# A new prologue order with token tiles normalised on GpSimd, and a new tile table

## The chip, the core and the metric

The kernel runs on one core of one Trainium2 chip. The core has a matrix engine (TensorE, PE in the profile; PEld is its weight load), VectorE (DVE), ScalarE (ACT), GpSimd (POOL) and SyncE (SP), which here only starts transfers. SBUF is the working memory, PSUM the memory of eight banks into which PE writes. The metric is the device time of one execution in microseconds (us). Three runs of the kernel before took 742.13, 742.68 and 742.68.

## The reference

One layer normalisation feeds two branches that are added to the input: attention with 32 query heads and a single key and value head (16 wide), and a dense layer with gelu.

```python
def _A_ref(x, wq, wk, wv, wo):                      # x is 1 x 2048 x 512
    H = 32; Dh = D // H                             # 16
    q = (x @ wq).reshape(B, S, H, Dh).transpose(0, 2, 1, 3)
    k = x @ wk
    v = x @ wv
    scores = jnp.einsum("bhqd,bkd->bhqk", q, k) * (Dh ** -0.5)
    p = _softmax(scores, axis=-1)
    o = jnp.einsum("bhqk,bkd->bhqd", p, v)
    return o.transpose(0, 2, 1, 3).reshape(B, S, H * Dh) @ wo

def _B_ref(x, w1, b1, w2, b2):                      # 512 -> 1792 -> 512
    h = _gelu(jnp.einsum("bsd,df->bsf", x, w1) + b1)
    return jnp.einsum("bsf,fd->bsd", h, w2) + b2

xn = _layernorm(x, axis=-1)
return x + _A_ref(xn, A_wq, A_wk, A_wv, A_wo) + _B_ref(xn, B_w1, B_b1, B_w2, B_b2)
```

The tensors are bfloat16. The output has to match within the usual error of bfloat16, which leaves room for an approximate exponential.

## The kernel before

*How it is planned.* The Python text first writes down every instruction with the engine, the buffers it reads and writes, an expected duration (`occ`), an expected latency until others see its result (`lat`) and, for some, a due time (`due`). Then `Prog.schedule` plays the five engines through in Python: each engine takes, among the instructions whose inputs are there, the one with the smallest due time (`min(cand, key=self.due)`), or, without one, with the smallest ready time plus `allow`. The order that comes out, and the waits between engines that it needs, are written into the program; on the chip every engine works through its own list in that order. So an edit of a due time or of an expected duration changes the order of instructions and nothing else. DMAs have a stream of their own and keep the due times written at their place.

*Main part.* Scores are made in 2048 tiles of 128 keys by 512 queries (4 query blocks x 8 head groups x 16 key tiles x 4 heads). Three tiles make a unit (683 units), one PSUM bank each; two halves of six banks are used in turn. `scores` (L984) is PE's product of KT and QT. A unit's tiles are then exponentiated either by ACT (`exp`, L1007, all its tiles of the unit in one instruction of 512 columns a tile) or, one tile in 3.6, by DVE with an approximation: `p1` (L1038) turns scores into int16 in `Dt`, and `close_batch` makes three more shifted copies of a batch of up to six tiles. Two of the three additions are DVE instructions over the whole batch (L1085), the third is one instruction a tile (L1081) that the planner puts on GpSimd or DVE. PE multiplies a tile of ACT with V once and a tile of DVE five times, with five scaled copies of V (L1051). `DTAB` has a letter for each unit that says which of its tiles go to DVE; the letters o, t, A, B and X also close the batch. `HP` and `YP` are the units at which the dense layer's two products are placed between the scores, as side work of PE (L681) whose results DVE takes out of PSUM.

*Prologue.* Before the first scores everything below has to be there; token tiles are 128 rows of x, sixteen of them, loaded in eight transfers.

1. Statistics of a token tile: on DVE, `bn_stats` and `bn_aggr` (L770, L784), or on ACT in two passes with accumulators (L767, L777). `LN_B` groups the tiles and says who does it ('d' or 'a').
2. For each group ACT computes the reciprocal deviation as exp(-0.5 ln(var)): L789, L791. Where ACT will normalise a tile, GpSimd makes the negated mean and its product first (`nm`, `nmr`, L773, L788, L793).
3. The normalised tile in `xn` (a part of `ub`, eight slots): `XN_ENG` has one letter a tile, ACT (L803) or DVE (L806, L809).
4. PE transposes a tile in four pieces (L821) into a PSUM bank; pairs of tiles (`TR_B`) are copied to `xnT` by ACT (L826) or DVE (L828) in one instruction of 128x1024.
5. PE projects keys (`K_B`, copied to KT by ACT, L840), and keys and values a token tile at a time (`v_tiles`). ACT squares the keys (L851, L855) and DVE reduces them (L852); the maximum over all keys (L908, L909, L911) goes through PE to `ibi` (L913), a bound that the scores of every row need.
6. The first query group: PE, then a copy (L865) and a square (L866) on DVE; with `ibi` DVE finishes QT (L872). The first `scores` wait for that.
7. DVE copies V out of PSUM (L919, L921) and GpSimd writes its five scaled copies (L925). GpSimd also writes all constants, zeroes QT (L719) and V1 (L733), and copies the first weights (L721, L886).

Due times of the prologue are given before as landing time of the tile (`LAND`) plus a constant for the kind of instruction (`DU`).

Of the kernel before, what the change touches and what calls it, by code (L numbers as in the profile page):

```python
# [64 lines left out]
DTAB = "oto00t0t..2otttt.0o.022t2tt22o.t0t.o.t0.o.2o200.t2.oo2t.o2o20.ooo0.0.2o2ot.00o2t0.00.20200t.2.oo.t202t0o22.22t.2tt.0.2o2o2.0o00.00oot.t2ooot0.00o.2oot.2oo002o.2tt.02ot.2t20..2t2t22t22xxXB2tt0.otot02to.0o02o0.0.o002tt202.2ttt..o0o20t22t0.0020o2t0202.20o0.o.tt.t.202o.t0o00o2o..o2tt22t22.2t.000o.20t..022tt2..0t.0t00t2t0.02o22.t02tt22.2o0.0o..to.22Bo..2to.0to0to.0oot020t0o2o22..tot00o.o0002o0t..02ot00o22..tt2020o202.oo0o.0202..oo20o0to.2to0.000t.2.o22to00o00.o2.t00o22.20.2tt..02o0022ot..202o.0o02t0ooo.220tot22ABXXB.ttt2o000o22..o0t22o.t0t2o2.o2o0ot02..2t0t222o2o.ot0.t0t2.0.t2o2o0o20o.202t0t2.0..2tt2o.2.to0.B0o0oo.0020t2t20t.t02o.2o0t0t..020o2o22ttt.t22t..ot2.t22t.222to.0oo.2.t.."  # L65
# [14 lines left out]
HP = ((53.36313,15,65.7807,136.33728,36.21312,67.40194,19.02609,18.84758,51,110.61621,34.41429,141,69.06988,99.66158),(149.70144,81.67117,82.37987,103.81985,165,0,0,0,0,0,0,0,0,0),(275.55645,309,280.33349,316.4732,250.53442,309,294.19346,284.369,335.7432,441.67367,320.02286,269.73972,453.75804,500.42149),(465.20765,488,484.21727,494.32464,439.21827,0,0,0,0,0,0,0,0,0))  # L80
YP = ((190.97923,183,219.34307,231),(345.97678,369.69708,381,411.01734),(538.21525,518.41703,557.35214,582.08895),(589.35156,621,652.22097,657))
# [9 lines left out]
Q_DUE = 16.0  # L91
# [4 lines left out]
XN_ENG = "adddddadddddaadd"  # L96
LN_B = (((0,), 'd'), ((1,), 'a'), ((2, 3, 4), 'd'), ((5,), 'a'), ((6, 7), 'd'), ((8, 9, 11), 'd'), ((13,), 'a'), ((14, 15), 'd'), ((10,), 'd'), ((12,), 'd'))
TR_B = (((0, 2), 2, 'a'), ((2, 4), 0, 'a'), ((4, 6), 1, 'd'), ((6, 8), 0, 'a'), ((8, 10), 0, 'd'), ((10, 12), 2, 'a'), ((12, 14), 1, 'a'), ((14, 16), 0, 'd'))
K_B = (((0, 2), 4), ((2, 6), 4), ((6, 10), 4), ((10, 12), 4), ((12, 16), 4))
V_B = ((0, 4), (4, 8), (8, 14), (14, 16))  # L100
NVA = 14
KV_ORD = (1, 2, 3, 4, 0)
# [444 lines left out]
def bass_parallel_sum__grouped_kv_mqa__dense_activation_gelu__prompt_kernel(  # L547
# [33 lines left out]
    with ExitStack() as es:  # L581
# [248 lines left out]
        def tr(a, b):  # L830
            return [("xnT", ti) for ti in range(a, b)]
# [618 lines left out]
```

## Time and profile before

| | |
|---|---|
| Runs | 742.13, 742.68, 742.68 us, median 742.68 |
| Profiled execution | 742.0 us, of which the span from first to last instruction is 740.3 us |
| First exponential of ACT starts | 24.09 us after the span's start |
| Granted TensorE clock | 1.000 |
| Instructions | 22182 |

The profile is one execution, recorded by the hardware. A row of a group reads: line of the kernel, engine, operation, tile written <- tiles read, shapes, count, then busy time, mean nanoseconds of one, and idle time of the engine before it with what ended it. A row of the order of time reads: start, duration, engine, line, operation, names, shapes, count. A row of a stretch gives its bounds and length, then busy time and count of instructions for PE, PEld, DVE, ACT and POOL, the granted clock, the share of the DMA engines and GB/s. The chain of waits follows the last instruction back to whatever released it, step by step, so a step's length there is the time until the next one could start, not the length of its record.

### The profile page before, as it was taken

To read this page: it belongs to the slowest core of one execution; us is meant where nothing else is said; L and a number is where in the kernel's file an instruction comes from. 1 tells how busy PE (TensorE), PEld (TensorE's weight loads), DVE (VectorE), ACT (ScalarE), POOL (GpSimd) and SP (SyncE) were. 2 spreads that over 40 slices of the span, in tenths; PEclk is the share of its full clock that TensorE was granted. 3 is DMA by queue.
4 is the path that set the end of the run, shared out by engine and by line. 5 is a ranking of instruction groups with operands and counts; after the bars stand their busy time and mean duration, and the time that the engine had idled before them with its cause. 6 is when DMAs were issued, how large, how long until landed. Compare 5 with 4: busy or idle time off the path is not lost.

```text
span 740.3 us, 22182 instructions
## 1 busy us (share of the span) xinstructions
PE 724.7 (98%) x9145; PEld 228.2 (31%) x9145; DVE 726.8 (98%) x1411; ACT 728.0 (98%) x759; POOL 393.7 (53%) x547
## 2 busy tenths in 40 slices
PE   7999999999999999999999999999999999999998
PEld 4323233222343223322232332232233222233222
DVE  8899999999999999999999999999999999999996
ACT  8999999999999999999999999999999999999997
POOL 5545565555415564555655546556643566644542
PEclk9999999999999999999999999999999999999999
DMA  9200100100020020101101010100100101101110
GB/s 312 67 15 16 33 8 17 25 10 20 10 48 15 5 54 17 26 23 30 25 13 35 25 39 18 24 23 9 26 17 20 30 23 38 31 24 25 27 25 27
DMA packets 36252, 23.57 MB, mean 32 GB/s; under 512 B 17768, under 2 KB 32568, under 8 KB 36152
## 3 DMA queue, kind: packets, MB, share of 16 engines
q1 hardware_dynamic: 35096, 22.12, 11.7%
q8 instruction: 73, 1.20, 0.7%
q14 instruction: 27, 0.22, 0.1%
q10 hardware_dynamic: 1056, 0.03, 0.1%
HBM read 13.28 MB, written 2.35 MB: 21 GB/s over the span
## 4 chain that ended last, share of the span: by engine, by line
ACT 63%; PE 32%; DVE 4%; DMA 0%; issue 0%; SPq 0%
ACT E L1007 62%; PE pAll L1051 15%; PE pAll L984 9%; PE pAll L681 7%; DVE stats L770 1%; DVE Dt L1038 1%; DVE Dt L1085 1%; DMA x_sb<-in_A_x_dram 0%; PE pAll L675 0%; DVE Dt L1081 0%; DVE ub L806 0%; ACT xnT L826 0%; ACT ub L803 0%; DVE Of L1132 0%; PE pAll L1411 0%
## 5 line engine op out<-in xcount | busy, mean ns | idle before, releaser
L1007 ACT ACTIVATE E<-pAll 128x1024 bf16<-128x1024 f32 (+1 forms) x678 | 675.2, 1191 | 2.3 <-PE pAll L984 2.2
L1081 POOL TENSOR_SCALAR Dt<-Dt 128x512 int16<-128x512 int16 x463 | 354.1, 765 | 311.2 <-DVE Dt L1085 137.3
L1051 PE MATMUL pAll<-Dt,V 128*32 128x512 bf16 x2850 | 422.4, 383 | 1.1 <-DVE Of L1132 1.1
L1038 DVE TENSOR_SCALAR Dt<-pAll 128x512 int16<-128x512 f32 (+1 forms) x555 | 377.3, 696 | 1.9 <-PE pAll L984 1.1
L1085 DVE TENSOR_SCALAR Dt<-Dt 128x1024 int16<-128x1024 int16 (+7 forms) x542 | 294.4, 571 | 0.1
L1051 PE MATMUL pAll<-E,V 128*32 128x512 bf16 x1478 | 276.0, 385 | 0.8 <-DVE Of L1132 0.8
L984 PE MATMUL pAll<-QT,KT 32*128 32x512 bf16 x2048 | 267.2, 384 | 4.4 <-ACT E L1007 2.8
L984 PEld LDWEIGHTS pAll<-QT,KT 32*128 32x128 bf16 x2048 | 66.5, 90 | 275.0 <-ACT E L1007 261.4
L1051 PEld LDWEIGHTS pAll<-Dt,V 128*32 128x32 bf16 x2850 | 112.4, 95 | 117.0 <-issue 70.9
L681 PE MATMUL pAll<-xnT,w_sb 128*32 128x512 bf16 x896 | 118.9, 382 | 0.0
L1051 PEld LDWEIGHTS pAll<-E,V 128*32 128x32 bf16 x1478 | 65.1, 94 | 51.3 <-issue 37.4
L681 PE MATMUL pAll<-w_sb,ub 128*32 128x512 bf16 x448 | 70.3, 382 | 0.0
L681 PE MATMUL pAll<-w_sb,x_sb 128*32 128x512 bf16 x448 | 68.4, 382 | 0.0
L681 PEld LDWEIGHTS pAll<-xnT,w_sb 128*32 128x32 bf16 x896 | 33.6, 95 | 21.1 <-issue 9.7
L681 PE MATMUL pAll<-wop,oTp 128*32 128x512 bf16 x192 | 31.4, 384 | 0.0
L1081 DVE TENSOR_SCALAR Dt<-Dt 128x512 int16<-128x512 int16 x107 | 27.5, 284 | 0.0
L1160 POOL TENSOR_TENSOR oTp<-OfP,rbP 128x256 bf16<-128x256 f32 x24 | 18.7, 790 | 7.5 <-DVE Dt L1085 3.9
L1215 DVE TENSOR_SCALAR ub<-pAll,b1T 128x512 bf16<-128x512 f32 x28 | 20.8, 742 | 0.2
L681 PE MATMUL pAll<-xnT,wq_sb 128*32 128x512 bf16 x256 | 20.0, 383 | 0.3 <-DVE ub L1215 0.3
L681 PEld LDWEIGHTS pAll<-w_sb,x_sb 128*32 128x32 bf16 x448 | 18.2, 95 | 4.8 <-issue 2.7
L681 PEld LDWEIGHTS pAll<-w_sb,ub 128*32 128x32 bf16 x448 | 18.5, 95 | 3.8 <-issue 2.0
L1132 DVE COPY Of<-pAll 128x512 f32<-128x512 f32 x24 | 16.3, 681 | 0.0
(122 smaller groups left out, 255.9 us busy)
## 6 DMA issues: line engine op xcount, KB each, us to landing
w_sb<-in_B_w_dram SPq DMA_DIRECT2D x2, 1792.0 KB, 13.2
OfP<-Of SPq DMA_DIRECT2D x96, 32.0 KB, 2.0
rbP<-rden_rows SPq DMA_DIRECT2D x96, 32.0 KB, 1.8
x_sb<-in_A_x_dram SPq DMA_DIRECT2D x8, 256.0 KB, 4.3
x_sb<-in_A_x_dram SPq DMA_DIRECT2D x16, 128.0 KB, 2.3
QT<-qp SPq DMA_DIRECT2D x124, 16.0 KB, 1.8
out_dram<-x_sb SPq DMA_DIRECT2D x15, 128.0 KB, 2.0
OfP<-Of SPq DMA_DIRECT2D x56, 16.0 KB, 1.8
```

Of the source, the lines that this page charges most:

```text
L681: add("pe", lambda e, c=c, j=j: e.matmul(o[c, :], l[:, c], rh, start=start, stop=stop, tile_position=(0, 32 * j)), r, [(k, j) for k in w] ...
L770: dve(lambda e, ti=ti, c=c: e.bn_stats(stats[:, c, :], x_sb[:, ti, :]), r=[("x", ti)], w=[("st", ti)], n=511, due=land(ti) + DU["sd"])
L984: ins = e.matmul(o, l, rh, start=True, stop=True, tile_position=(q0, 0))
L1007: o = act(lambda e: e.activation(E[:, s0:s0 + na, :], bank(b0, na).rearrange("p (a n) -> p a n", a=na), ACT.Exp, scale=LN2 / 128.0), w=[B( ...
L1038: op = dve(lambda e: e.tensor_scalar(Dt[:, s:s + n, :], bank(bk, n).rearrange("p (a n) -> p a n", a=n), float(127 * 128) + SPL_D, SPL_MIN, ...
L1051: add("pe", lambda e, a, b: e.matmul(pO[32 * j:32 * j + 32, :], V1[:, v, kt, :], rhs, start=a, stop=b, tile_position=(0, 32 * j)), r=r + [ ...
L1081: add("pool", lambda e, d=d, k=k: e.tensor_scalar(d, d, 1.0, float(k), ALU.mult, ALU.add), [], [(("D", base[o > 0] + q), o)], occ=PL_OCC, ...
L1085: dve(lambda e, d=view(o, nb), q=view(i, nb), k=k: e.tensor_scalar(d, q, float(k), None, ALU.add), r=keys(i), w=keys(o), n=nb * n * TBW, m ...
L1132: dve(lambda e: e.tensor_copy(Of[:, i, :], pO), w=["O", ("Of", i)], allow=0.0)
L1160: "pool", lambda e, c=c: e.tensor_tensor(oTp[0:n, sl, c], OfP[0:n, s, c], rbP[0:n, s, c], ALU.mult),
L1215: dve(lambda e: e.tensor_scalar(ubs[tb % 2][:, ft, :], pM, b1T[:, ft:ft + 1], None, ALU.add), r=["b1T"], w=M4 + [ukey(tb, ft)], n=TBW + 57 ...
```

## The change

All in one edit:

- `XN_ENG` gets a third letter, p, for GpSimd: eleven tiles are normalised there, two on ACT (4 before), three on DVE (12 before).
- `LN_B`: thirteen groups instead of ten; two tiles instead of three have their statistics on ACT.
- `TR_B`: the copies to `xnT` are on ACT for two pairs, on DVE for four; the last two pairs are split ('s'), half of the columns by each of them from two banks. Keys of `xnT` in the planner become halves, so that PE can start a projection on the first half.
- `K_B` groups the keys by 4, 2, 2, 4, 4 tiles (before 2, 4, 4, 2, 4). `NVA` is 10 instead of 14: the squared keys are reduced in two pieces by DVE.
- The first QT copy goes to ACT (`Q_ENG`), the zeroing of QT is split between DVE and GpSimd (`Q0_SPLIT`), one of the five scaled V copies goes to DVE (`KV_DVE`).
- Every instruction ahead of the first scores gets a due time of its own (`PRO_DUE`, 308 numbers, set by the new `rank`); `DU` and the due times written at the instructions are gone. Expected durations and latencies of the prologue are changed.
- `DTAB`, `HP` and `YP` are replaced by other tables.

In the old table 570 tiles go to DVE, in 271 batches (99 of one tile, 92 of two, 47 of three, 23 of four, 6 of five, 4 of six); in the new one 571, in 250 batches (83, 79, 47, 26, 5, 10). Both leave ACT 678 instructions. 418 of the 683 letters differ.

```diff
-DTAB = "oto00t0t..2otttt.0o.022t2tt22o.t0t.o.t0.o.2o200.t2.oo2t.o2o20.ooo0.0.2o2ot
...
+DTAB = "2to00o2.o0.t0222t.o.0to200t.22.0o020.o0.t.2t000o2.t.2t000t.o002.o020.202.o
...
-XN_ENG = "adddddadddddaadd"
-LN_B = (((0,), 'd'), ((1,), 'a'), ((2, 3, 4), 'd'), ((5,), 'a'), ((6, 7), 'd'), ((8, 9, 11), 'd'), ((13,), 'a'), ((14, 15), 'd'), ((10,), 'd'), ((12,), 'd'))
-TR_B = (((0, 2), 2, 'a'), ((2, 4), 0, 'a'), ((4, 6), 1, 'd'), ((6, 8), 0, 'a'), ((8, 10), 0, 'd'), ((10, 12), 2, 'a'), ((12, 14), 1, 'a'), ((14, 16), 0, 'd'))
-K_B = (((0, 2), 4), ((2, 6), 4), ((6, 10), 4), ((10, 12), 4), ((12, 16), 4))
-NVA = 14
-KV_ORD = (1, 2, 3, 4, 0)
-KV_DVE = ()
+XN_ENG = "papppdpppppdapdp"
+LN_B = (((0,), "d"), ((1,), "a"), ((2, 3), "d"), ((4,), "a"), ((5,), "d"), ((6,), "d"), ((7, 12), "d"), ((8,), "d"), ((9,), "d"), ((11,), "d"), ((13,), "d"), ((10, 14), "d"), ((15,), "d"))
+TR_B = (((0, 2), 1, "d"), ((2, 4), 0, "a"), ((4, 6), 2, "d"), ((6, 8), 1, "a"), ((8, 10), 1, "d"), ((10, 12), 2, "d"), ((12, 14), 0, "s"), ((14, 16), 0, "s"))
+K_B = (((0, 4), 4), ((4, 6), 4), ((6, 8), 4), ((8, 12), 4), ((12, 16), 4))
+NVA = 10
+KV_ORD = (4, 1, 0, 3, 2)
+KV_DVE = (2,)
+XP_OCC = 0.75
+PRO_DUE = (10.3,11.34,29.84,9.77,-0.16,19.38,19.64,19.9,13.73,13.99,14.25,11.64
...
+Q_ENG = "ad"
+Q0_SPLIT = 4
...
+    def rank(self):
+        s0 = next(o.idx for o in self.ops if o.kind == "S")
+        due = iter(PRO_DUE)
+        for op in self.ops[:s0]:
+            op.due = (op.due or 0.0) if op.stream != op.eng else next(due)
+
     def schedule(self):
         ops = self.ops
+        self.rank()
...
+        for g0, g1, f, kw in ((0, Q0_SPLIT, dve, dict(n=Q0_SPLIT * TBW // 2)), (Q0_SPLIT, NGR, setup, dict(occ=0.24 * (NGR - Q0_SPLIT)))):
+            if g0 < g1:
+                f(lambda e, g0=g0, g1=g1: e.memset(QT[:, g0:g1, :].rearrange("p g n -> p (g n)").bitcast(f32), 0.0),
...
+                f = lambda e: e.tensor_scalar(xn[:, ti % 8, :], x_sb[:, ti, :], mean, rs, o, ALU.mult)
+                rw = dict(r=[("x", ti), ("rstd", b), key], w=[("u", 0, ti % 8)])
+                if XN_ENG[ti] == "p":
+                    setup(f, occ=XP_OCC, **rw)
+                else:
+                    dve(f, n=245, **rw)
...
+            parts = ((0, 2, bk, "a"), (2, 4, (bk + 1) % 3, "d")) if eng == "s" else ((0, DT, bk, eng),)
+            for d0, d1, bk, eng in parts:
+                m = (d1 - d0) * n
+                pT = bank(bk)[:, 0:m * 64].bitcast(bf)
...
+            if Q_ENG[0] == "a":
+                act(lambda e: e.activation(QT[:, 0, :], bank(bk), ACT.Copy), w=[B(bk)] + q_rows(0))
```

More of the change, by code (lines that the diff above doesn't have):

```diff
@@ L659, in B @@
             return ("bank", b)
-        dlat = [0.16, 0.23]
+        dlat = [0.135, 0.2]
         def dve(fn, r=(), w=(), n=TBW, mode=1, allow=1.0, **kw):
@@ L907, in bass_parallel_sum__grouped_kv_mqa__dense_activation_gelu__prompt_kernel @@
                 q_first(7)
-        dve(lambda e: e.tensor_reduce(kmx[:], kmax[:], AX.X, ALU.max), r=[("kmax", 0), ("kmax", NVA)], w=["kmx"], n=40, due=0.0)
+        dve(lambda e: e.tensor_reduce(kmx[:], kmax[:], AX.X, ALU.max), r=[("kmax", ti) for ti in range(NT)], w=["kmx"], n=40, due=0.0)
         add("pe", lambda e: e.transpose(bank(3)[0:1, 0:P], kmx[:], ident_f[:]), r=["kmx", "ident_f"], w=[B(3)], occ=0.12, lat=0.22,
```

146 lines of the change are left out of this document (70 added, 76 removed).

## The prediction

> **What bounds the kernel now.** I read the totals first, then the stretches of time, then the chain of waits through the start, then single engines by shape.
>
> ```profile
> PE 724.7 (98%) x9145; PEld 228.2 (31%) x9145; DVE 726.8 (98%) x1411; ACT 728.0 (98%) x759; POOL 393.7 (53%) x547
> ...
> 24.00:733.00 709.00, 703.01 (x8909) 215.49 (x8910) 706.04 (x1349) 706.29 (x703) 381.25 (x499) 1.00 0.10 23
> ```
>
> Three engines are busy 98% each; the second row (PE, PEld, DVE, ACT, POOL in that order) says that from 24 to 733 us VectorE (DVE) and ScalarE (ACT) leave under 3 us open. Busy time alone does not name the bound, since records of neighbours overlap. The order of time of DVE shows by how much:
>
> ```profile
> 399.49 0.68 DVE L1038 TENSOR_SCALAR Dt<-pAll 128x512 int16<-128x512 f32 x1
> 400.09 0.28 DVE L1085 TENSOR_SCALAR Dt<-Dt 128x512 int16<-128x512 int16 x1
> 400.29 0.68 DVE L1038 TENSOR_SCALAR Dt<-pAll 128x512 int16<-128x512 f32 x1
> 400.89 0.41 DVE L1085 TENSOR_SCALAR Dt<-Dt 128x1024 int16<-128x1024 int16 x1
> 401.22 0.68 DVE L1038 TENSOR_SCALAR Dt<-pAll 128x512 int16<-128x512 f32 x1
> ```
>
> A 0.68 record is followed after 0.60, a 0.28 after 0.20, a 0.41 after 0.33: a step is the record less 0.08, and the next instruction starts at that moment each time. So DVE is truly full in the main part, and what is taken from its work there comes off the time. ACT has a little hidden air: one exponential of 128x1024 costs it 0.87 when fed, as PE's releases show (an ACT of one unit frees the next group of scores at 726.83 and again at 727.70), against a mean of 675.2/678 = 0.996 per instruction.
>
> ```profile
> L1007 ACT ACTIVATE E<-pAll 128x1024 bf16<-128x1024 f32 (+1 forms) x678 | 675.2, 1191 | 2.3 <-PE pAll L984 2.2
> ...
> 726.83 0.10 PEld L984 LDWEIGHTS pAll<-QT,KT 32*128 32x128 bf16 x3 [0.42 <-ACT E L1007]
> ...
> 727.70 0.10 PEld L984 LDWEIGHTS pAll<-QT,KT 32*128 32x128 bf16 x3 [0.42 <-ACT E L1007]
> ```
>
> Ahead of it lies a prologue in which no attention tile can start: all sixteen token tiles must be normalised, transposed and projected, since the row bound is a maximum over all keys. By stretches and by the chain:
>
> ```profile
> 0.00:5.00 5.00, 3.26 (x16) 2.26 (x16) 1.47 (x5) 2.19 (x4) 4.31 (x19) 1.00 0.64 161
> 5.00:10.00 5.00, 2.93 (x22) 2.01 (x21) 5.00 (x15) 4.72 (x15) 4.25 (x20) 1.00 1.10 348
> 10.00:15.00 5.00, 3.91 (x63) 2.82 (x61) 5.00 (x15) 5.00 (x14) 1.30 (x7) 1.00 1.03 398
> 15.00:20.00 5.00, 4.30 (x59) 2.62 (x55) 4.51 (x13) 4.85 (x14) 0.52 (x2) 1.00 1.10 352
> ...
> 7.56 0.08 DVE mv L784
> 7.64 0.58 DVE stats L770
> ...
> 8.68 0.95 DVE ub L806 x3
> ...
> 16.19 0.29 ACT lnv L789
> ...
> 17.19 0.09 ACT rstd L791
> 17.29 0.70 ACT ub L803
> 17.99 1.82 ACT xnT L826 x2
> ...
> 22.79 0.81 DVE QT L872
> ...
> 24.09 0.70 DVE Dt L1038
> ```
>
> From 5 to 20 us DVE and ACT are full and GpSimd (POOL) is nearly empty after 10. The chain runs along DVE (statistics 0.58 + 0.08 a tile, a normalised tile 0.95/3 = 0.317), at the end over ACT, and the first exponential and the first L1038 start together at 24.09. Whatever pulls that moment forward moves everything behind it.
>
> **The change part by part.** *Prologue, DVE.* Nine of its twelve normalised tiles go to GpSimd (letters d: 12, then 3): 9 x 0.317 = -2.85. The copy of the first QT goes to ACT:
>
> ```profile
> 16.69 0.69 DVE L865 CAST QT<-pAll 128x512 bf16<-128x512 f32 x1
> ...
> 17.29 0.68 DVE L828 COPY xnT<-pAll 128x1024 bf16<-128x1024 bf16 x1
> ```
>
> so -0.60 (16.69 to 17.29). Added: one tile of statistics moves from ACT to DVE, +0.66; the copies of xnT out of PSUM on DVE go from three whole ones to four and two halves, a whole one 0.68 less the 0.08, so +0.60, a half about 0.34 (an estimate: half of it and a fixed part), so +0.68; a second small reduce of kmax, about +0.15 (an estimate: the shortest DVE records beside it are 0.17). Sum -3.45 + 2.09 = -1.36, call it -1.4. The zeroing of half of QT (128x1024) comes to DVE too; a 128x256 memset took 0.27 there, so about 1.1, and it lies in the 2.4 us in which DVE waits for the first tokens. If that cover were gone, it would cost its 1.1.
>
> ```profile
> 1.20 0.27 DVE L718 MEMSET oTp<- 128x256 uint32 x1
> ...
> 3.87 0.69 DVE L770 BATCH_NORM_STATS2 stats<-x_sb 128x6 f32<-128x512 bf16 x1 [2.40 <-DMA x_sb<-in_A_x_dram]
> ```
>
> *Prologue, ACT.*
>
> ```profile
> L777 ACT ACTIVATE oTp<-x_sb,nm 128x512 bf16<-128x512 bf16 x3 | 2.1, 710 | 0.0
> ...
> 21.45 0.17 DVE L908 TENSOR_REDUCE kmx<-kmax 128x1 f32<-128x16 f32 x1
> ```
>
> Two normalised tiles fewer (-2 x 0.70), one tile of statistics fewer (two passes like L777, -1.4), copies out of PSUM from five whole ones (1.82/2 = 0.91 each) to two and two halves (near -1.8), against three more pairs of logarithm and exponential (thirteen groups for ten, 0.29 + 0.09 each, +1.1) and the QT copy (+0.6): about -2.9. ACT falls by more than DVE, so DVE sets the prologue and I count its -1.4. The bounds: 0 if the new order leaves as much new idle as work goes; -2.2 if DVE runs gapless from the second pair of tokens (statistics of before began at 4.95): it then has 13 statistics (8.6), 3 tiles (0.95) and copies (3.1) left, the last copy ends near 17.6, and an estimated 1.6 us of projection, square and reduce bring the key maximum (L908) to 19.2, where it started at 21.45.
>
> *Prologue, GpSimd.* No row has this operation (pointer scalars, bf16 to another tile). The nearest is the same instruction on 512 two-byte elements; farther ones are 256 f32 elements in short rows (L925, 0.93 apart) and a pointer scalar on 128 elements (L932).
>
> ```profile
> L1081 POOL TENSOR_SCALAR Dt<-Dt 128x512 int16<-128x512 int16 x463 | 354.1, 765 | 311.2 <-DVE Dt L1085 137.3 <-PE pAll L1051 59.0 <-DVE Dt L1038 49.4
> ...
> 21.81 4.65 POOL L925 TENSOR_SCALAR V<-oTp 128x256 bf16<-128x256 f32 x5 [5.31 <-DVE oTp L919]
> ...
> 5.14 0.20 ACT L791 ACTIVATE rstd<-lnv 128x1 f32<-128x1 f32 x1
> ...
> L932 POOL TENSOR_SCALAR sel8R<-sel,R x1: 887/887/887, 26.4 to 26.4; 128x128 bf16<-128x128 bf16 x1
> ...
> L1081 POOL TENSOR_SCALAR Dt<-Dt x463: 619/621/1797, 28.0 to 729.1; 128x512 int16<-128x512 int16 x155
> ```
>
> Bounds: 0.62 (median, alone) and 2.95 (if 0.2 of the 0.887 is fixed, 0.69 for 128 elements, times four, plus 0.2). I take the mean 0.77, since width, element size and two arithmetic steps agree with it. Eleven tiles are 8.5; the small steps between them and the two weight copies are about 1.8 (an estimate, nine records of 0.2); the set-up work that GpSimd did by 10 us was 8.56, less 0.9 for the half QT, of which 4.5 fit ahead of the first reciprocal deviation (L791, 5.14 + 0.20), so 3.2 are left over. From 5.3 this ends at 5.3 + 8.5 + 1.8 + 3.2 = 18.8 at worst, and near 15.6 if the left-over set-up stands behind. The transposes of the last tiles are queued behind it on PE. The last normalised tiles of before ended at 18.95, so GpSimd hides, with little to spare. No DMA is added and none moved.
>
> *End of the prologue.* One of five scaled copies of V goes from GpSimd (0.93 apart) to DVE and may stand between the small steps there, beside GpSimd's other copies: 0 to 0.9, taken +0.3. The dues, the latencies of the planner and the moved memset of epsc change no instruction; they cost nothing but order, which the bounds above hold.
>
> *Main part.* The tile letters give 571 instead of 570 tiles to DVE; the count of ACT's exponentials stays 678 and one tile less is worth at most 0.4 there. A batch of tiles on DVE ends with two additions (L1085); the letters make 250 batches of 271, so 42 instructions fewer.
>
> ```profile
> L1085 DVE TENSOR_SCALAR Dt<-Dt 128x1024 int16<-128x1024 int16 (+7 forms) x542 | 294.4, 571 | 0.1
> ...
> L1085 DVE TENSOR_SCALAR Dt<-Dt 128x2048 int16<-128x2048 int16 x115 | 78.2, 683 | 0.0
> L1085 DVE TENSOR_SCALAR Dt<-Dt 128x1024 int16<-128x1024 int16 x191 | 77.6, 418 | 0.1
> ...
> L1081 DVE TENSOR_SCALAR Dt<-Dt 128x512 int16<-128x512 int16 x107 | 27.5, 284 | 0.0
> ```
>
> (542 = 2 x 271 bears the count out.) From 1024 to 2048 elements a record grows by 0.265, so 0.153 is fixed, 0.073 of it after the overlap: 42 x 0.073 = -3.1. The added tile costs 0.60 (L1038) and 3 x 0.133 (its share of the additions) = +1.0. DVE's balance is -2.1, and DVE is the full engine. What the table does besides is not in the rows: the third kind of addition, L1081, ran 463 times on GpSimd and 107 times on DVE at 0.20 a step, split by the planner; 20 more or fewer on DVE are +-4. Larger batches also hold DVE longer at a time (a 3072 step instead of a 1024 one) while a score bank waits to be emptied. I take -1.8, a little less than the balance, with -6 and +3 as bounds. The new places of the projection groups (HP, YP) move work of PE and DVE within the same count: inside those bounds.
>
> *Sum.* -1.4 + 0.3 - 1.8 = -2.9. The profiled execution took 742.0 (span 740.3, 1.7 around it): 739.1. The median of the runs, 742.68, lies 0.7 above the profiled one: **739.8**.
>
> **A rule to weigh.** L1081 on GpSimd takes 0.62 alone, yet up to 1.80, and the long ones stand beside DVE's L1085:
>
> ```profile
> 439.72 1.26 POOL L1081 TENSOR_SCALAR Dt<-Dt 128x512 int16<-128x512 int16 x1 [0.18 <-DVE Dt L1038]
> ...
> 439.56 0.95 DVE L1085 TENSOR_SCALAR Dt<-Dt 128x3072 int16<-128x3072 int16 x1
> ```
>
> The statistics, copies out of PSUM and casts showed no such thing, but GpSimd was at work beside only a part of them. The Trainium skill ("SBUF — State Buffer", "Who interferes with whom") says that GpSimd and a VectorE instruction which uses both SBUF ports, or has two SBUF inputs, shut each other out for a whole instruction. By that rule DVE's three own normalised tiles, the square of QT and the small copies of V would stand behind GpSimd's tiles. The trace agrees for L1081 and cannot show it for the new pairing. The first rival prices it from rows.
>
> **The rivals.** *GpSimd's tiles hold up DVE in the prologue (11%).* The instructions in question are about seven (three tiles, one square, three copies into V1). Each can wait up to the 0.62 of a GpSimd tile, half of it on average: 7 x 0.31 = 2.2 in place of the 0.3: -1.4 + 2.2 - 1.8 = -1.0, so 741.7. For: the pair above. Against: statistics are most of DVE's work there, and nothing in their thirteen records varied.
>
> *The prologue comes, the table gives nothing (17%).* DVE's saving goes into waits on late scores. For: DVE and ACT waited only 3 us in 709, so nearly any other order has more to lose than to win. Against: fewer instructions on the full engine. -1.4 + 0.3 = -1.1: 741.6. If besides 23 additions of L1081 come to DVE (8%), +4.6 - 2.1 more: +1.4, 744.1.
>
> *GpSimd is too slow for eleven tiles (slower, 8%).* Place: its queue, from the first deviation at 5.3 to the last tile; everything behind it, transposes, projections, key maximum, waits. Price: with c us a tile it ends at 5.3 + 1.8 + 11c when the set-up stands behind. It decides against the change from 18.95 + 1.8 on (the old end and the main part's saving), c = 1.24. At c = 1.5 it ends at 23.6, 4.65 later than before: +4.65 - 1.8 = +2.85, 745.5. For: L932, whose rate gives 2.95, and L925, 0.93 for half the elements. Against: 463 records of the same width at 0.62 to 0.77; L932 also ran beside two L1085.
>
> *More than the sum (14%).* DVE runs gapless to the maximum (-2.2), no copy of V is in the way, the table gives its -2.1 and the last piece of KT, which ACT did after the first exponential before, falls into ACT's idle time of the final chain (about -0.6): -4.9, 737.8.
>
> That the change doesn't do what it says has no room: the engine letters and the batches are fixed in the text.
>
> **How the numbers follow.** The sum gets 42%: 739.8, its own range 738.3 to 741.2. The limit of what can be told here is 0.2%, 1.5 us: faster is under 741.2, slower above 744.2. Faster: 42 + 14, and of the two cases near 741.6 about a third (10) = 0.66. Slower: 8 from GpSimd, half of the 8 at 744.1, and 2 for waits dearer than I priced = 0.14. Same: 0.20. The range reaches from the lower bound of the gapless case with some of L1081 leaving DVE, 736.9, to 744.0, which leaves out GpSimd's case and the far ends of the table.
>
> **What would show it.** Right: L908 near 19.5 to 20.2 and the first L1007 and L1038 near 23.0; GpSimd's eleven tiles at 0.62 to 0.8 apart, its last before 17; DVE full from 5 to 19 with 14 statistics; L1085 x500 and DVE still under 3 us idle after the start. Wrong: GpSimd tiles over 1.2; DVE records of copies or additions stretched beside them; L1081 on DVE far from 107 times; more idle of ACT before scores (2.2 us now). The forecast falls if the first exponential moves by less than 0.5 or if the time from it to the end grows.

## The result and the profile after

| | before | after |
|---|---|---|
| Median of the runs | 742.65 us (4 runs, 742.13 to 742.68) | 753.95 us (4 runs, 753.80 to 754.08) |
| Ratio | | 1.0154, interval 1.0136 to 1.0171 |
| Profiled execution, span | 742.0, 740.3 | 754.08, 752.4 |
| First exponential | 24.09 | 36.68 |
| First exponential to the end of the span | 716.21 | 715.72 |

The kernel became 11.3 us slower; 739.8 with a range of 736.9 to 744.0 had been forecast. The lower two rows place it: the start lost 36.68 - 24.09 = 12.59, the rest gained 0.49, together the 12.1 between the spans.

The changed kernel by stretches (bounds and length, then busy time and count of PE, PEld, DVE, ACT and POOL, granted clock, DMA share, GB/s).

```profile
5.00:10.00 5.00, 1.61 (x10) 1.30 (x11) 4.86 (x13) 3.09 (x13) 5.00 (x11) 1.00 1.09 352
10.00:15.00 5.00, 2.33 (x19) 1.31 (x18) 3.94 (x12) 2.22 (x8) 5.00 (x6) 1.00 1.03 398
15.00:20.00 5.00, 2.58 (x30) 1.72 (x28) 0.20 (x1) 1.90 (x5) 5.00 (x7) 0.54 1.10 349
20.00:25.00 5.00, 3.78 (x44) 2.63 (x43) 2.34 (x7) 3.47 (x12) 5.00 (x6) 0.77 0.37 114
25.00:30.00 5.00, 2.44 (x29) 1.71 (x28) 1.56 (x4) 0.90 (x2) 5.00 (x3) 0.91 0.01 2
```

Before, DVE and ACT were nearly full from 5 to 20 and GpSimd was nearly empty from 10. Now GpSimd is full for 25 us without a gap; from 15 to 20 DVE works 0.20 of the 5 us and TensorE 2.58, at a granted clock of 0.54. The chain of waits through the start (start, time until the next step could begin, what) is GpSimd's list of tiles:

```profile
10.43 6.14 POOL ub L817 x3
...
16.88 2.76 POOL ub L817 x2
...
22.07 2.06 POOL ub L817
...
24.47 6.17 POOL ub L817 x3
...
30.69 0.61 PE pAll L836 x4
...
36.68 0.69 DVE Dt L1057
```

L817 is the normalised tile. The view of that line alone gives the duration of one (least, median, greatest in ns), and who waited for it:

```profile
L817 POOL TENSOR_SCALAR ub<-x_sb,mv,rstd x10: 2062/2066/2094, 6.2 to 28.6; 128x512 bf16<-128x512 bf16 x10
L817 DVE TENSOR_SCALAR ub<-x_sb,mv,rstd x3: 406/412/430, 11.3 to 25.2; 128x512 bf16<-128x512 bf16 x3
L817 POOL TENSOR_SCALAR ub<-x_sb,nm,rstd x1: 758/758/758, 18.9 to 18.9; 128x512 bf16<-128x512 bf16 x1
...
  PEld pAll L836: 15.2, 9
  PE pAll L836: 12.3, 7
```

Ten tiles took 2.07 each and one took 0.76, of the same size, type and buffers. The odd one is tile 4, whose statistics ACT makes: it gets the negated mean (`nm`) and the pair of operations (add, mult); the ten get the mean (`mv`) and (subtract, mult). The transposes (L836) wait for them.

### The profile page after: what moved, and what is told of

It reads as the page before. It is cut to its first block, busy times and chain, and to the rows that moved or that the text cites. A ratio compares the mean times of both kernels' runs of the same rounds, so it can differ in the third digit from the quotient of the medians.

```text
span 752.4 us, 22198 instructions
## 1 busy us (share of the span) xinstructions
PE 730.7 (97%) x9173; PEld 238.1 (32%) x9173; DVE 727.6 (97%) x1376; ACT 724.9 (96%) x756; POOL 419.1 (56%) x546
## 4 chain that ended last, share of the span: by engine, by line
PE 50%; ACT 38%; DVE 7%; POOL 4%; DMA 0%; issue 0%
ACT E L1026 38%; PE pAll L1070 25%; PE pAll L1003 16%; PE pAll L689 9%; DVE Dt L1057 3%; POOL ub L817 3%; DVE Dt L1104 2%; PE pAll L1430 1%; DMA wvk<-in_A_wk_dram 0%; PE pAll L683 0%; DVE Dt L1100 0%; DVE ub L1234 0%; DVE x_sb L1234 0%; DVE Of L1151 0%; POOL V L743 0%
## 5 line engine op out<-in xcount | busy, mean ns | idle before, releaser
L1100 POOL TENSOR_SCALAR Dt<-Dt 128x512 int16<-128x512 int16 x457 | 360.4, 789 | 312.4 <-DVE Dt L1104 154.2
L1057 DVE TENSOR_SCALAR Dt<-pAll 128x512 int16<-128x512 f32 x557 | 381.1, 700 | 1.6 <-PE pAll L1003 0.9
L1104 DVE TENSOR_SCALAR Dt<-Dt 128x1024 int16<-128x1024 int16 (+6 forms) x500 | 294.1, 614 | 0.1
L1070 PE MATMUL pAll<-E,V 128*32 128x512 bf16 x1477 | 283.8, 385 | 0.0
L689 PE MATMUL pAll<-xnT,w_sb 128*32 128x512 bf16 x896 | 115.3, 382 | 0.0
L689 PE MATMUL pAll<-w_sb,x_sb 128*32 128x512 bf16 x448 | 64.8, 381 | 0.0
L689 PE MATMUL pAll<-wop,oTp 128*32 128x512 bf16 x192 | 36.6, 384 | 0.0
L817 POOL TENSOR_SCALAR ub<-x_sb,mv,rstd 128x512 bf16<-128x512 bf16 x10 | 20.7, 2071 | 0.0
L836 PE MATMUL pAll<-ident,ub 128*128 128x128 bf16 x64 | 7.9, 268 | 12.9 <-POOL ub L817 12.3
```

Of the source, the lines that this page charges most:

```text
L689: add("pe", lambda e, c=c, j=j: e.matmul(o[c, :], l[:, c], rh, start=start, stop=stop, tile_position=(0, 32 * j)), r, [(k, j) for k in w] ...
L817: f = lambda e: e.tensor_scalar(xn[:, ti % 8, :], x_sb[:, ti, :], mean, rs, o, ALU.mult)
L836: add("pe", lambda e, ti=ti, d=d, o=o, pT=pT: e.transpose(pT[:, o:o + P], xn[:, ti % 8, d * P:(d + 1) * P], ident[:]), r=[("u", 0, ti % 8) ...
L1057: op = dve(lambda e: e.tensor_scalar(Dt[:, s:s + n, :], bank(bk, n).rearrange("p (a n) -> p a n", a=n), float(127 * 128) + SPL_D, SPL_MIN, ...
L1070: add("pe", lambda e, a, b: e.matmul(pO[32 * j:32 * j + 32, :], V1[:, v, kt, :], rhs, start=a, stop=b, tile_position=(0, 32 * j)), r=r + [ ...
L1100: add("pool", lambda e, d=d, k=k: e.tensor_scalar(d, d, 1.0, float(k), ALU.mult, ALU.add), [], [(("D", base[o > 0] + q), o)], occ=PL_OCC, ...
```

## The experiments

Two theories for the 2.07: the pair of operations sets GpSimd's price; or its place does, a tile that reads `mv` and shares SBUF with a busy DVE being held up. The stretch from 15 to 20 already speaks against the second, since a tile took 2.07 there beside an idle DVE.

**The same instruction with add in place of subtract.** The order of all engines is that of the changed kernel. The mean is added instead of subtracted.

```diff
                 if XN_ENG[ti] == "p":
+                    f = lambda e: e.tensor_scalar(xn[:, ti % 8, :], x_sb[:, ti, :], mean, rs, ALU.add, ALU.mult)
                     setup(f, occ=XP_OCC, **rw)
```

> The changed kernel, but the GpSimd tiles use (add, mult) with the same two pointer scalars where it has (subtract, mult), so the mean is added and not subtracted; the planned order, the waits and the addresses stay as they are. Theory A, the price of a GpSimd tile hangs on the operation: all eleven take 0.76 us as tile 4 did, first exponential at 22.5 to 23.5 us instead of 36.68, time 740.5 to 741.6. Theory B, it hangs on where the mean lies (every second word of mv, against nm for tile 4): ten tiles stay at 2.07 and the time at 754. Theory C, it is neighbours on the shared port: they stay long wherever DVE is at work, some way between.

Measured: 741.31 us (10 runs; before beside it 742.26), ratio 0.9988, interval 0.9979 to 0.9997. The view of the line, a row of the order of time, and the stretch from the first exponential to the end:

```profile
L820 POOL TENSOR_SCALAR ub<-x_sb,mv,rstd x10: 757/766/904, 6.4 to 17.5; 128x512 bf16<-128x512 bf16 x10
L817 DVE TENSOR_SCALAR ub<-x_sb,mv,rstd x3: 415/557/594, 10.3 to 17.1; 128x512 bf16<-128x512 bf16 x3
```

```profile
21.04 0.16 DVE L929 TENSOR_REDUCE kmx<-kmax 128x1 f32<-128x16 f32 x1
...
21.64 0.27 PE L930 MATMUL pAll<-ident_f,kmx 128*1 128x128 f32 x1
...
24.06 2.85 ACT L1027 ACTIVATE E<-pAll 128x1024 bf16<-128x1024 f32 x3
```

```profile
24.06:739.60 715.54, 708.51 (x8986) 224.36 (x8986) 708.18 (x1323) 707.55 (x708) 387.33 (x491) 1.00 0.10 23
```

One word of the instruction is worth 12.6 us (36.68 to 24.06 at the first exponential). The address read is the same, DVE is busier than in the changed kernel (4.32 of the 5 us from 15 to 20, where it was 0.20), and the tile takes 0.77: the pair of operations it is. The same run shows a second thing: with the tiles at the price that the prediction took, the first exponential comes at 24.06 and not near 23.0, and the rest takes 715.54 instead of 716.21. The forecast gain is not there either; that is taken up below.

**Which pairs are cheap.** Two kernels give each of the eleven GpSimd tiles a pair of its own, so the tiles hold no normalised values; only their durations are read.

```diff
+PAIRS = {0: ("subtract", "mult", 0.5, 2.0), 2: ("mult", "add", None, None), 3: ("mult", "subtract", None, None), ...
+                    o1, o2, s1, s2 = PAIRS.get(ti, ("subtract", "mult", mean, rs))
```

> The changed kernel with nine of the ten (subtract, mult) tiles of GpSimd given other pairs of operations or immediate scalars (tile 0 subtract and mult with two immediates, 2 mult and add, 3 mult and subtract, 6 subtract with an immediate, 7 add and mult, 8 add and mult with immediates, 9 subtract pointer and mult immediate, 10 add and add, 13 subtract and subtract; tile 15 as it was), so nine tiles are not normalised. Theory A: every pair with subtract takes near 2.07, every pair of add and mult near 0.76 or less, whatever the scalars are. Theory B: pairs with the pointer into mv take 2.07, add included. Third: only the exact pair (subtract, mult) is slow, then 3 and 13 are fast.

> As the first run of pairs, with others on GpSimd's tiles (0 mult and mult, 2 add alone, 3 mult alone, 4 add and mult, 6 subtract alone, 7 mult and add, 8 add and subtract, 9 max and add, 10 mult and max, 13 subtract and add, 15 subtract and mult), so most tiles are not normalised. The first run had 0.61 to 0.76 for (add, mult) and (mult, add), but 2.12 for (add, add) and near 2.0 wherever subtract was. Theory: only a pair of one add and one mult is fast: tiles 4 and 7 near 0.76, all other pairs near 2.0. Single operations: open, 0.6 if they are done as a pair with a neutral partner, else 1.3 to 2.

Measured, the order of time of GpSimd in the first; its queue has the tiles in the order 0, 3 and 2 (one row), 6, 7, 4, 8, 9, then 10, 13, 15 (one row):

```profile
6.19 1.96 POOL L824 TENSOR_SCALAR ub<-x_sb 128x512 bf16<-128x512 bf16 x1
10.17 2.84 POOL L824 TENSOR_SCALAR ub<-x_sb,mv,rstd 128x512 bf16<-128x512 bf16 x2
13.01 2.00 POOL L824 TENSOR_SCALAR ub<-x_sb,rstd 128x512 bf16<-128x512 bf16 x1
15.26 0.76 POOL L824 TENSOR_SCALAR ub<-x_sb,mv,rstd 128x512 bf16<-128x512 bf16 x1
16.01 2.07 POOL L824 TENSOR_SCALAR ub<-x_sb,nm,rstd 128x512 bf16<-128x512 bf16 x1
18.22 0.61 POOL L824 TENSOR_SCALAR ub<-x_sb 128x512 bf16<-128x512 bf16 x1
```

(subtract, mult) of two constants takes 1.96, of a constant and a pointer 2.00, of `nm` 2.07: neither the pointers nor the address matter much. (add, mult) takes 0.76, and with constants 0.61. In the second:

```profile
6.22 0.77 POOL L824 TENSOR_SCALAR ub<-x_sb,mv,rstd 128x512 bf16<-128x512 bf16 x1
9.00 4.70 POOL L824 TENSOR_SCALAR ub<-x_sb,mv 128x512 bf16<-128x512 bf16 x3
...
15.53 2.07 POOL L824 TENSOR_SCALAR ub<-x_sb,mv,rstd 128x512 bf16<-128x512 bf16 x1
```

(mult, mult) takes 0.77, which the second expectation had among the slow ones; one operation alone (mult, add, subtract) takes 4.70/3 = 1.57, twice the price of a cheap pair; (add, subtract) takes 2.07. Together:

| Operations on GpSimd, 128x512 bf16 | us |
|---|---|
| (add, mult), (mult, add), (mult, mult) | 0.76 to 0.77; (mult, add) with one constant 0.69, (add, mult) with two 0.61 |
| one alone: add, mult, subtract | 1.56 to 1.59 |
| (subtract, mult), (mult, subtract), (subtract, subtract), (subtract, add), (add, subtract), (add, add), (mult, max), (max, add) | 1.96 to 2.12 |

The Trainium skill ("GPSIMD Engine Reference", "3.1 Elementwise — side-by-side cycle accounting") gives 769 ns for 512 elements as the best case of an elementwise loop. The trace agrees for three pairs with pointers, at 757 to 771 ns. With constants two of them lie under that best case, at 609 and 687 ns, and the other pairs lie far over it, at 1.96 to 2.12 us; here the measurement decides.

**Negated means.** Eight small instructions make the negated mean of the tiles that DVE has statistics of, and every GpSimd tile is (add, mult). In the first form the order of all engines is planned anew, in the second the order of the changed kernel is kept and the eight are put into GpSimd's list afterwards.

```diff
-                if any(XN_ENG[ti] == "a" for ti in ts):
+                if any(XN_ENG[ti] in "ap" for ti in ts):
...
                     setup(lambda e: e.tensor_scalar(nm[:, sl], mv[:, sl, 0], -1.0, None, ALU.mult), r=sk, w=[("nm", b)], occ=0.17, **kw)
...
-                mean, key, o = (mv[:, c, 0:1], ("mv", ti), ALU.subtract) if how == "d" else (nm[:, c:c + 1], ("nm", b), ALU.add)
+                mean, key, o = (mv[:, c, 0:1], ("mv", ti), ALU.subtract) if how == "d" and XN_ENG[ti] == "d" else (nm[:, c:c + 1], ("nm", b), ALU.add)
```

> The changed kernel with a negated mean for every GpSimd tile (nine more small GpSimd instructions, 0.15 to 0.2 us each) and (add, mult): the same result as the reference's. Theory A: tiles at 0.76, first exponential at 22.7 to 24, time 740.3 to 742, so a little faster than before or the same. Theory B and C: the time stays at 750 or above, or comes down by less than half of the 11.3.

> The changed kernel's planned order kept for every engine, GpSimd tiles as (add, mult), and eight small GpSimd instructions for the negated means put into GpSimd's list afterwards, without planning anew; the same result as the reference's. Theory A with the order of the main part as a second cause (the +26 of the run with newly planned negated means came from the new order, not from the eight instructions): first exponential 24.0 to 24.7, time 741.2 to 742.2, so 0 to 1 under before. Rival: the small instructions themselves cost the 26 in GpSimd's queue: 750 or more.

Measured: planned anew 768.70 us, ratio 1.0355 (1.0341 to 1.0370), although the first exponential comes at 27.04; the time from there to the end is 739.9, some 24 more. With the order kept 742.31, ratio 1.0002 (0.9993 to 1.0011), first exponential 25.04, the rest 715.5. The first form is no test of the negation. Its time is over 750, as the theories of place and neighbours had it, but not for their reason: its GpSimd tiles take 0.76, and a new order of the main part, with the same tables, costs 24 us. The second is a test: eight instructions in GpSimd's queue delay the start by 25.04 - 24.06 = 0.98, a little more than expected.

**The table alone.** The kernel before with the new `DTAB`, `HP` and `YP`, and the kernel with added means with the old ones.

```diff
-DTAB = "oto00t0t..2otttt.0o.022t2tt22o.t0t.o.t0.o.2o200.t2.oo2t.o2o20.ooo0.0.2o2ot
...
+DTAB = "2to00o2.o0.t0222t.o.0to200t.22.0o020.o0.t.2t000o2.t.2t000t.o002.o020.202.o
...
-HP = ((53.36313,15,65.7807,136.33728
...
+HP = ((51.20561,31,67,144.42454
```

> The kernel before with the new tile table and the new places of the projections alone; its prologue unchanged. My forecast for the main part: -1.8, so 740.9. The changed kernel's trace says -0.5 from the first exponential to the end, so 742.1. Rival: the tables fit only the prologue they were made for and cost 1 to 3 with the old one, 743.6 to 745.6.

> The new prologue with (add, mult) tiles, as in the run that adds the mean (so tiles are not normalised rightly), with the OLD tile table and projection places. If a table fits only the prologue it was found with: first exponential near 24 but a main part 15 to 35 longer, 757 to 777, with more L1081 on DVE than 114 and ACT waiting for PE's products with V. If the new table is better in itself by 0.5 to 1.8: 742 to 743.5.

Measured: 775.14 us (ratio 1.0442, 1.0428 to 1.0456) and 779.72 us (1.0499, 1.0485 to 1.0513). The first lies some 30 us over all that was expected of it; the second is the loss that was expected if a table fits one prologue only, and 3 us more.

| | old table | new table |
|---|---|---|
| old prologue | 742.3 | 775.14 |
| new prologue, (add, mult) | 779.72 | 741.31 |

The view of waits for the kernel before with the new table (engine, line, what it waited for: us in all, times, longest):

```profile
ACT E L1007 <- PE pAll L1051: 20.0, 11, 5.6
ACT E L1007 <- PE pAll L984: 5.5, 13, 0.9
```

and for the kernel before:

```profile
ACT E L1007 <- PE pAll L984: 2.2, 5, 0.5
```

The exponentials stand still for 20 us behind the accumulation of p times V (L1051), in eleven waits that the right partner doesn't have. DVE has more to do as well. The group of single additions that the planner puts on DVE, in the kernel before with the new table:

```profile
L1081 DVE TENSOR_SCALAR Dt<-Dt 128x512 int16<-128x512 int16 x184 | 46.3, 287 | 0.0
```

It has 184 of them, 201 with the new prologue and the old table, and 186 where the order was planned anew with negated means, against 107 and 114 with the right partner. At the 0.20 a step that the prediction read from the rows, 77 more are some 15 us (an estimate) on an engine that was full. Which of the two comes first, the waits or the additions, no run separates. The new table has its 250 batches with either prologue, and its worth goes from -38 to +33: the effect of prologue and table isn't a sum. In these four kernels a table fits the order that it was found with.

**What holds the start now, and where the eight instructions belong.** Three kernels, run beside one another: the negated means on DVE (the order kept), the kernel with added means once more, and the same with the key projection of tiles 8 to 11 cut, whose keys are then not computed.

```diff
+                    (lambda f, occ, **k: dve(f, n=15, **k) if own else setup(f, occ=occ, **k))(lambda e: e.tensor_scalar(nm[:, sl], mv[:, sl, 0], -1.0, None, ALU.mult), ...
```

```diff
+                n1 = 8 if ts[0] == 8 else n
-                mm(bank(bk)[:, 0:n], wkp[:, d, :, :].rearrange("p a n -> p (a n)"), xnT[:, d, c], d == 0, d == DT - 1,
+                mm(bank(bk)[:, 0:n1], wkp[:, d, :, :].rearrange("p a n -> p (a n)"), xnT[:, d, ts[0] * P:ts[0] * P + n1], d == 0, d == DT - 1,
```

> The changed kernel with its plan kept and every GpSimd tile as (add, mult), fed by negated means that eight small instructions on DVE make (the output is the reference's); the run before this one had the same eight on GpSimd, in its queue between the tiles. Theory (GpSimd's queue sets the prologue from the first tile on, so eight small instructions there cost 1.0 us; DVE has room between its statistics): the first exponential comes at 24.1 to 24.6, the time is 741.4 to 742.0, the main part (first exponential to the end of the span) stays at 715.5. Rival (DVE is what sets the prologue, as the prediction had it): eight instructions of some 0.06 to 0.1 us on DVE push the key maxima by 0.5 to 0.8, so first exponential 24.6 to 25.0 and 742.0 to 742.4, no better than with them on GpSimd.

> The kernel whose GpSimd tiles add the mean, once more and unaltered, to stand beside the two others of this call on the same chip: 741.2 to 741.4 by its first ten runs, first exponential at 24.06. A difference of over 0.2 us from the first call would mean that differences of that size between calls are not read.

> The kernel whose GpSimd tiles add the mean (741.31, first exponential at 24.06), with the key projection of token tiles 8 to 11 cut from 512 columns to 8, so that the keys of these tiles aren't computed; nothing else is changed. Theory (TensorE is what sets the prologue's last 3 us once GpSimd's tiles are short: four key projections of 1.04 us stand in its queue ahead of the transpose that the key maxima wait for): that transpose comes 0.3 to 0.5 earlier, the first exponential at 23.6 to 23.7, the time 740.8 to 741.0. Rival (the chain through DVE, or the copies after the projections of tiles 12 to 15, sets it): the first exponential stays at 24.0 to 24.1 and the time at 741.2 to 741.4.

Measured: means on DVE 741.53 us (11 runs, ratio 0.9992, 0.9983 to 1.0001), first exponential 24.42, the rest 715.48; added means again 741.44; cut projection 741.36. Before stood at 742.19. The first exponential of the first lies where the theory has it, 24.42 - 24.06 = 0.36 later, where GpSimd's queue lost 0.98. The theory's reason, room on DVE, does not hold, as the stretch from DVE's first statistics to the key maxima shows (us; bounds from the order of time, busy time from the stretches):

| Kernel | Stretch | Length | DVE busy | GpSimd busy |
|---|---|---|---|---|
| before | 3.87 to 21.45 | 17.58 | 16.36 | 7.20 |
| new prologue, added means | 4.16 to 21.04 | 16.88 | 15.74 | 13.53 |
| negated means on DVE | 4.07 to 21.40 | 17.33 | 16.24 | 13.67 |
| negated means on GpSimd | 4.16 to 22.02 | 17.86 | 16.05 | 14.88 |

The eight add 0.50 to DVE's work and lengthen the stretch by 0.45; on GpSimd they add 1.35 and lengthen it by 0.98. Most of the work comes through on either engine. DVE is the better place because the eight are shorter there (median 138 ns against 208).

For the third, the kernel with the cut projection:

```profile
21.09 0.25 PE L683 MATMUL pAll<-xnT,oTp 128*128 128x8 bf16 x4 [0.19 <-ACT KT L856]
...
21.56 0.16 DVE L930 TENSOR_REDUCE kmx<-kmax 128x1 f32<-128x16 f32 x1
...
21.78 0.27 PE L931 MATMUL pAll<-ident_f,kmx 128*1 128x128 f32 x1 [0.19 <-DVE kmx L930]
...
24.32 1.94 ACT L1028 ACTIVATE E<-pAll 128x1024 bf16<-128x1024 f32 x2
```

and the uncut one beside it:

```profile
21.34 1.04 PE L683 MATMUL pAll<-xnT,oTp 128*128 128x512 bf16 x4 [0.19 <-ACT KT L855]
...
21.81 0.16 DVE L929 TENSOR_REDUCE kmx<-kmax 128x1 f32<-128x16 f32 x1
...
22.43 0.27 PE L930 MATMUL pAll<-ident_f,kmx 128*1 128x128 f32 x1
...
24.85 1.94 ACT L1027 ACTIVATE E<-pAll 128x1024 bf16<-128x1024 f32 x2
```

With full projections of tiles 8 to 11 in TensorE's queue the transpose of the key maxima (L930) starts 0.62 after the maxima, without them 0.22. From the projections to the first exponential it is 3.51 against 3.23. So the queue does hold the start, by 0.28. The time doesn't follow: 0.08 between the medians is within their spread, and in the profiled executions the rest takes 715.78 instead of 715.45. The 0.3 to 0.5 that was expected of the time is a miss, and where the 0.28 is given back was not looked for further.

The uncut kernel was the same text as the first of these experiments, yet its profiled execution had its first exponential at 24.85 and not at 24.06, and took 742.07. TensorE's order of time in the two executions, the late one first, and the late one's stretches show what differs:

```profile
7.23 0.40 PE L837 MATMUL pAll<-ident,ub 128*128 128x128 bf16 x4 [2.78 <-POOL ub L820]
7.46 1.15 PE L1429 MATMUL pAll<-zeros 128*128 128x256 bf16 x9
10.05 0.61 PE L837 MATMUL pAll<-ident,ub 128*128 128x128 bf16 x4 [1.44 <-ACT ub L813]
```

```profile
7.64 2.13 PE L1429 MATMUL pAll<-zeros 128*128 128x256 bf16 x9
10.05 0.61 PE L837 MATMUL pAll<-ident,ub 128*128 128x128 bf16 x4 [0.29 <-ACT ub L813]
```

```profile
8.00:9.00 1.00, 0.61 (x6) 0.29 (x3) 1.00 (x4) 0.96 (x7) 1.00 (x3) 0.74 1.11 351
...
14.00:15.00 1.00, 1.00 (x9) 0.98 (x9) 0.15 (x1) 1.00 (x4) 0.50 (x3) 0.50 1.01 395
15.00:16.00 1.00, 1.00 (x11) 0.53 (x9) 0.93 (x4) 0.91 (x3) 1.00 (x2) 0.84 1.05 360
```

In the late execution TensorE's clock was granted at 0.50 from 8.5 to 15.3 (not to 15.8, as the next expectation has it). The idle time from 4.4 to 7.2 cannot be the whole reason, since the first execution has it too (2.79). What differs is the pace behind it. The late one ran the nine products of zeros in 1.15, then idled for 1.44, and its clock fell. The other one needed 2.13 for the same nine and idled for only 0.29. Its clock column reads 1.00 throughout, but 2.13 for nine is the pace of the first fifteen (3.38 in both), so the column cannot be taken at its word this early. The executions of 741.84 to 742.17 (5 of the 21 of this text) are exactly those with a mean clock of 0.995; the others lie at 740.82 to 741.53.

**Keeping TensorE busy.** The kernel with means on DVE, plus 18 more of the products of zeros with which the kernel fills TensorE's idle time, 12 and 6 of them behind the first two groups.

```diff
+        ends = [a for a, b in zip(pe, pe[1:]) if a.kind == "fill" and b.kind != "fill"]
+        for a, k in zip(ends, (12, 6)):
+            for _ in range(k):
...
+                order.insert(order.index(a) + 1, f)
```

> The kernel with negated means on DVE (741.53) plus 18 more products of zeros on TensorE in its two idle stretches of the prologue, 12 behind the first 15 (idle from 4.4 to 7.2) and 6 behind the next nine (idle from 8.6 to 10). Theory (in some executions TensorE's granted clock falls to 0.50 from about 8.5 to 15.8 because it was idle there, and such an execution ends 0.7 later): no execution shows a mean clock of 0.995 any more and none lies near 742.1; the others stay at 741.3 to 741.6, so the median is 741.4 and the highest of some eleven under 741.9. First exponential 24.3 to 24.5. Rival (the late executions come from something else, or the fillers stand in the way of the first transposes): two or three of eleven still at 742.0 to 742.2, or all of them 0.1 to 0.3 later.

> The kernel with negated means on DVE once more, unaltered, beside the one with more products of zeros: median 741.5, and two or three of eleven executions at 742.0 to 742.2 with a mean clock of 0.995, as in the first call (9 at 741.34 to 741.75, 2 at 742.18 and 742.20).

Measured: with the products 741.49 us (11 runs, before 742.27; ratio 0.9994, 0.9985 to 1.0003), none of eleven with a clock of 0.995; without them 742.14 (ratio 0.9996, 0.9987 to 1.0005), five of eleven with 0.995 (two or three were expected), at 742.14 to 742.37, where the undisturbed ones lie at 741.47 to 741.64. In the first call of this kernel two of eleven had 0.995, so seven of its 22 in all. The stretches of the kernel with the products, where TensorE now works from 5 to 7:

```profile
5.00:6.00 1.00, 1.00 (x7) 0.69 (x6) 0.86 (x4) 0.50 (x2) 1.00 (x1) 1.00 1.08 323
6.00:7.00 1.00, 0.64 (x5) 0.29 (x3) 1.00 (x2) 0.55 (x1) 1.00 (x3) 1.00 1.10 368
```

So none of the executions with the products shows the 0.995 any more. Late ones there still are, against the expectation that none would exceed 741.9: three at 742.54 to 742.64, which are exactly the three that read 0.998, all others reading 1.000. By an estimate from these figures 0.998 is some 3 us at half clock (0.002 x 740 / 0.5), so the clock may be behind them too; no trace shows where. But 0.998 also stands beside times like 741.34 in the first call, and one execution without the products took 742.57 at 1.000. Three late ones of eleven against six of eleven do not show that the products make late executions rarer. The median with the products is 12.5 under the changed kernel and 0.8 under the kernel before; the interval of the latter doesn't exclude that there is no difference.

## Why the prediction was wrong

- **The step that failed is GpSimd's price.** The prediction took 0.77 a tile "since width, element size and two arithmetic steps agree" with L1081; ten of the eleven took 2.07. L1081 multiplies by 1.0 and adds a constant, one of the three cheap pairs; the tile subtracts and multiplies. The operations themselves were what the row did not share. The bounds (0.62 to 2.95) held the measured value. The rows that spoke for a higher one, L932 and L925, are single multiplications, of the kind that takes 1.57 here; twice L925's 0.93 for half the elements, 1.86, would have been nearer, though by another operation. The choice within the bounds was made on traits that don't set the price.
- **"So GpSimd hides"** went with it. The rival with its condition was there, slower from c = 1.24, at 8%. Its own formula with the measured prices, 5.3 + 1.8 + 10 x 2.07 + 0.76 = 28.6, comes within 2.1 of the measured end of the last tile, 30.64; the first tile began at 6.26, not at 5.3. The mechanism was right, its chance was far too small, and the range stopped short of it.
- **Prologue -1.4.** Even with tiles of 0.77 the first exponential moved by 0.03, not by 1.1 (-1.4 and +0.3). Up to the key maxima DVE's busy time fell by 16.36 - 15.74 = 0.62, not by 1.4; the term that came out worst is the nine tiles, -2.4 start to start instead of -2.85, since DVE's other three became longer (the point on GpSimd holding DVE up). The stretch from the first statistics to the maxima shrank by 0.70. The first statistics began 0.29 later, a matter of the single execution: they begin at 3.87 to 4.22 in the profiles, at 3.88 in one with the new prologue and at 4.14 in one with the old. So the maxima came at 21.04 instead of 21.45, 0.41 earlier. The way from there to the first exponential grew from 2.64 to 3.02; the key projections queued ahead on TensorE hold it by 0.28, as shown above, and the prediction put nothing for that queue. "DVE sets the prologue" itself was not refuted: DVE is busy for 15.74 of the 16.88, and what was added to it came through to 0.45 of 0.50. GpSimd's queue had become as tight beside it.
- **Main part -1.8.** Measured 715.72 - 716.21 = -0.49, with the cheap tiles -0.67 (715.54). The busy time by groups of DVE, of the kernel with added means when it ran again, and of the one group of the kernel before that the prediction doesn't show:

```profile
L1058 DVE TENSOR_SCALAR Dt<-pAll 128x512 int16<-128x512 f32 x557 | 378.5, 694 | 1.7 <-PE pAll L1004 0.9
L1105 DVE TENSOR_SCALAR Dt<-Dt 128x1024 int16<-128x1024 int16 (+6 forms) x500 | 291.7, 607 | 0.1
L1101 DVE TENSOR_SCALAR Dt<-Dt 128x512 int16<-128x512 int16 x114 | 29.6, 283 | 0.0
```

```profile
L1038 DVE TENSOR_SCALAR Dt<-pAll 128x512 int16<-128x512 f32 (+1 forms) x555 | 377.3, 696 | 1.9 <-PE pAll L984 1.1
```

  A group's busy time leaves out only what neighbours of the same group overlap, so the three are compared as the prediction counted, by count times mean less 0.08. The batches came as counted: 542 x 0.491 = 266.1 became 500 x 0.527 = 263.5, so -2.6, close to the prediction's -3.1 and, for the extra tile, +0.4. But seven more single additions landed on DVE: 107 x 0.204 = 21.8 became 114 x 0.203 = 23.1, +1.3. L1058 grew by 0.1 (555 x 0.616 to 557 x 0.614) where 0.6 had been counted. The balance is -1.2 instead of -2.1; the term that was left at 107 "+-20" took back half of what the batches gave. The stretch from the first exponential to the end of the kernel before shows what was left of that for the engine as a whole:

```profile
24.09:740.30 716.21, 707.27 (x8970) 217.04 (x8968) 708.10 (x1356) 708.93 (x708) 381.15 (x499) 1.00 0.10 23
```

  DVE is busy for 708.10 there and for 708.18 with the new tables, so its other groups took up the 1.2; which ones was not followed. ACT's 708.93 became 707.55. That ACT's 1.4 less is what gave the 0.67 is a reading of these rows; no run tests it. The prediction's "hidden air" on ACT, 0.87 against a mean of 0.996, sets one width against a mean over three (128 of the 678 exponentials are 128x1536); the sum did not use it.
- **The sum itself.** Prologue and table were added as if each had a worth of its own. The four kernels of the square above show that they have none apart: 33 and 38 us lie between right and wrong partners. The prediction's bounds of -6 and +3 for the table would have been far too narrow for the old prologue; its rival "nearly any other order has more to lose than to win" named it.
- **GpSimd holding DVE up** (the rival at 741.7) was there and small: two of DVE's three tiles took 0.56 and 0.59 beside cheap GpSimd tiles, the third 0.41, so 0.33 in all, not 2.2; with the negated means on GpSimd two took 0.72 and 0.74. The square and the copies of V were not looked at. The Trainium skill ("SBUF — State Buffer", "Who interferes with whom") states that exclusion for a VectorE instruction in the modes that use both ports, which a tensor_scalar can enter; the trace agrees with 0.41 against 0.59 here and 0.74 there. The 2.07 has nothing to do with it, since a tile took that beside an idle DVE.
- **What would show it** pointed at the right rows: GpSimd tiles over 1.2 and a first exponential that doesn't come earlier were both named as signs against the forecast.

## What to carry to other kernels

Price an instruction that the trace doesn't have by a row with the same engine, the same shape and the same operations; where the operations differ, the bounds have to weigh as much as the value. On GpSimd write a subtraction as an addition of a negated value, and make that value where it costs least: 0.36 on DVE against 0.98 on GpSimd here. Tables and orders found together are kept or dropped together: the time of one with another partner does not tell its worth.

## What the hardware showed unexpectedly

- One tensor-scalar instruction on GpSimd costs 0.61 to 0.77, 1.57 or about 2.07 for the same 128x512 elements of two bytes, by its operations (constants in place of pointers change 0.76 to 0.61 and 2.07 to 1.96); the two operations (mult, add) together are cheaper than either one of them alone.
- The same text ran TensorE at a granted clock of 0.50 for some 7 us of the prologue (8.5 to 15.3) in part of the executions (5 of 21; 7 of 22 with the means on DVE) and not in the others. In the one of them that has a trace, an idle stretch of 2.78 and one of 1.44, with 1.4 of work between them, came ahead of it or at its start. The Trainium skill ("TensorE: Matmul & The Clock Gate", "What's actually happening") says that the clock follows an activity window of about 3.4 us that runs freely of the kernel's start, so that the same kernel differs from run to run in its first products. The trace agrees in that the nine products of zeros take 1.15 in one execution and 2.13 in another of the same text. With the added products none of eleven executions had such a clock.
